# Chunked attention and two MoE layers on one core: a TensorE order written by hand at the entry, earlier weight transfers, and the column sums of w_out as matrix products

## The chip, the cores and the metric

The kernel runs on one core of one Trainium2 chip. The metric is the time of one execution in device microseconds; the profile comes from one profiled execution on the same kind of core. In the profile PE is TensorE's matrix products and PEld its weight loads, DVE is VectorE, ACT is ScalarE, POOL is GpSimd, and SP is the queue that issues most DMA transfers.

## The reference

Three layers follow each other. Chunked attention over 3072 tokens (4 batches of 768, 8 heads of 64): each chunk of 32 queries sees 16 keys to its left, its own 32, 8 to its right, and 8 memory keys. Its output, 3072 rows of 512, goes through a dense layer with 2048 hidden features, and that through a layer of 8 experts in which each token is assigned to one expert, each expert taking exactly 384 tokens.

```python
def _moe_ref(x, w_in, w_out, s, b):
    h = x @ w_in
    r = np.maximum(h, 0.0)
    g = s * (r * r) + b
    return (g @ w_out).astype(np.float32)
```

The dense layer is the one that the change is about. `w_in` and `w_out` come as float64. Since `b` is added to each of the hidden features, its share of the output is `b` times the column sums of `w_out`, one row of 512 numbers for all tokens.

## The kernel before

Tokens go in 24 tiles of 128, and two tiles make a group of 256 columns; there are twelve groups.

Attention of one tile (`stages`, from line 180) is a chain between the engines: TensorE transposes keys (`pk`) and queries (`pq`), ScalarE copies them (`kT`, `qT`), VectorE and ScalarE set up the key windows (`kwin`), TensorE makes the scores (`sc`), VectorE takes maxima and subtracts (`mx`, `sm`), ScalarE takes the exponential, TensorE transposes (`pp`), ScalarE copies (`pT`), TensorE multiplies with the values (`po`, from the buffers `vw`), VectorE divides (`den`, `xr`), TensorE transposes (`px`), ScalarE rounds the result (`xT` high part, line 240) and VectorE keeps the remainder (`xT` low part, line 241).

The dense layer works in units (group, f), f from 0 to 15, each for 128 hidden features. `gemm1` makes twelve matrix products of 256 columns (line 316, tile `ph`: four slices of the model dimension, and for each high times high, high times low, low times high). ScalarE takes relu (line 319), square and rounding; VectorE keeps the low part `g` (line 324). `gemm2` adds the unit into the two output tiles of its group with six products of 512 columns (line 345), three units later (LAG). `ph` comes from a PSUM pool with two buffers, the output tiles from one with four.

The weights arrive as float64 and are converted while the first units run (`convert`, line 265). A piece is 128 columns of `w_in` or 128 rows of `w_out`, 512 KB; there are 32, and three buffers `raw` hold them. For each, ScalarE makes a scaled copy `y` (line 277), VectorE does three integer operations (lines 278, 280, 281), ScalarE rounds the high part (line 262) and GpSimd subtracts for the low part (line 263). For pieces of `w_out` GpSimd also adds `y` into `wsum` (line 290), and one product with ones (line 397) sums that over the partitions once groups 0 and 1 are through.

Groups 0 and 1 run together, group 1 behind group 0, and from group 2 on the groups follow each other, with the attention of later tiles between. The order on TensorE is written out for tiles 0 and 1 only (`begin` in `manual_schedule`); behind that a scheduler places instructions by its own estimate of the times. The order of SP's transfers is written out through the whole entry (`begin`, `startup`, `feed`). All queues run in order: an instruction that waits holds everything behind it on its engine.

Of the kernel before, what the change touches and what calls it, by code (L numbers as in the profile page):

```python
# [18 lines left out]
P = 128  # L19
# [5 lines left out]
def kernel(ctx, tc, q, k, v, mem_k, mem_v, w_in, w_out, moe_s, moe_b,  # L25
# [33 lines left out]
    nc.gpsimd.memset(wsum, 0.0)  # L59
# [48 lines left out]

    vb = [None, None]
# [44 lines left out]
    def k_transpose(t):  # L154
        x = k_raw.pop(t)
        pk = psa[0].tile([P, HP, P], F32, tag="pa", name=f"pk{t}")
        for hp in range(HP):
            nc.tensor.transpose(pk[:, hp, :], x[:, 2 * hp:2 * hp + 2, :].rearrange("p h d -> p (h d)"), ident)
        kT[t] = at.tile([P, HP, P], F32, tag="kT", name=f"kT{t}", bufs=3)
        nc.scalar.activation(kT[t], pk, AF.Copy)  # L160

    def windows(t):
        b = t // TPB
# [3 lines left out]
        cp = (nc.vector if t < 2 * GT else nc.gpsimd).tensor_copy  # L167
        for c in (1, 2):
            nc.scalar.activation(kwin[:, :, c, 0:W], x[:, :, c * CH - LEFT:c * CH - LEFT + W], AF.Copy)
# [9 lines left out]

    def stages(t):  # L180
        first, last = t % TPB == 0, t % TPB == TPB - 1
# [6 lines left out]
        nc.scalar.activation(qT, pq, AF.Copy)  # L188
        windows(t)
        sc = [psa[0].tile([P, HP, KW], F32, tag="pa", name=f"sc{t}_{i}") for i in range(2)]  # L190
# [10 lines left out]
        for par in range(2):  # L201
            if first:
                nc.vector.memset(sc[par][0:CH, :, 0:LEFT], -1.0e30)
            if last:
                nc.vector.memset(sc[par][P - CH:P, :, W - RIGHT:W], -1.0e30)
            nc.vector.tensor_reduce(mx[:, par, :], sc[par], axis=AX.X, op=ALU.max)
            nc.vector.tensor_tensor(sm[:, :, par, :], sc[par],
                                    mx[:, par, :, None].to_broadcast([P, HP, KW]), op=ALU.subtract)
        nc.scalar.activation(sm, sm, AF.Exp, scale=scale)
# [4 lines left out]
        (nc.scalar.copy if t < 2 * GT else nc.vector.tensor_copy)(pT, pp)  # L214
# [12 lines left out]
        for par in range(2):  # L227
            nc.vector.tensor_scalar(den[:, par, :], po[par][:, :, D], 1e-9, None, op0=ALU.add)
        nc.vector.reciprocal(den, den)
        for par in range(2):  # L230
            nc.vector.tensor_tensor(xr[:, :, par, :], po[par][:, :, 0:D],
                                    den[:, par, :, None].to_broadcast([P, HP, D]), op=ALU.mult)
# [7 lines left out]
        nc.scalar.activation(hi, px, AF.Copy)  # L240
        nc.vector.tensor_tensor(lo, px, hi.bitcast(F32), op=ALU.subtract)
# [17 lines left out]
    st = sctx.enter_context(tc.tile_pool(name="st", bufs=2))  # L259

    def split(c, hi, lo, i):
        nc.scalar.activation(hi, c, AF.Copy)  # L262
        nc.gpsimd.tensor_tensor(lo, c, hi.bitcast(F32), op=ALU.subtract)

    def convert(src, a, n, hi, lo, i):

        if src.dtype == F32:
# [4 lines left out]
        raw = st.tile([P, a, n, 2], I32, tag="raw", name=f"raw{i}", bufs=3)  # L272
        nc.sync.dma_start(raw.rearrange("p a f w -> p a (f w)"),
                          src.bitcast(I32).rearrange("(a p) f -> p a f", p=P))
# [13 lines left out]
    def load_wout(f):  # L288
        y = convert(w_out[f * P:(f + 1) * P, :], 1, DM, wout_ap3(0, f), wout_ap3(1, f), 2 * f + 1)
        nc.gpsimd.tensor_tensor(wsum, wsum, y[:, 0, :], op=ALU.add)  # L290
# [18 lines left out]

    def gemm1(j, f):  # L310
        ph = ps_h.tile([P, GN], F32, tag="ph", name=f"ph{j}_{f}")
# [21 lines left out]
    def gemm2_(j, f):  # L333
        nonlocal ps_o, ps_l
        if (j, f) == (3, 0):
            octx.close()
            ps_o, ps_l = (actx.enter_context(tc.tile_pool(name=n, bufs=k, space=PSUM, reuse_waits="tile"))
                          for n, k in (("ps_o3", 3), ("ps_l", 1)))
# [54 lines left out]
    def load_wg():  # L393
        ones = xp[0].tile([P, P], F32, tag="x2", name="onesP")
        nc.vector.memset(ones, 1.0)
        ps = psa[0].tile([P, DM], F32, tag="pa", name="pws")
        nc.tensor.matmul(ps, ones, wsum, start=True, stop=True)
# [632 lines left out]
```

## Time and profile before

| | |
|---|---|
| time, median of 3 runs | 1112.98 us (1112.59 to 1114.03) |
| the profiled execution's own time | 1110.14 us |
| its span | 1108.4 us |
| TensorE busy | 1017.7 us, 92% |
| VectorE busy | 776.3 us, 70% |
| ScalarE busy | 474.1 us, 43% |
| GpSimd busy | 230.9 us, 21% |

A busy TensorE in this table is one whose products stand in its pipeline one behind the other; it may still run at a lower clock. The 8% in which it idles lies at the two ends of the program: in the first 140 us, where weights are still being converted, and in the last 400, where tokens are routed to the experts. The change is about the first.

### The profile page before, as it was taken

The page shows a single profiled execution, that of the slowest core. Times are in us where ns is not written, and L with a number is a line of the kernel's source. Part 1 is how long each engine was busy: PE and PEld are TensorE (multiplying, and loading weights), DVE is VectorE, ACT ScalarE, POOL GpSimd, SP SyncE. Part 2 cuts the span into 40 slices and gives each one's busy share as a digit, 9 for nine tenths or more (in the row PEclk, how much of TensorE's full clock was granted, in tenths as well). Part 3 has the DMA queues.
Part 4 walks back from the last instruction along what each step waited for, and adds up shares of the span by engine and source line. Part 5 has one row for each costly group of instructions (what it writes and reads, how often), then busy time and mean ns, then how long its engine had stood idle before and what let it go on. Part 6 is the DMA issues. An engine that isn't in the chain of part 4 may idle for free.

```text
span 1108.4 us, 25066 instructions
## 1 busy us (share of the span) xinstructions
PE 1017.7 (92%) x9397; PEld 889.8 (80%) x9397; DVE 776.3 (70%) x2979; ACT 474.1 (43%) x1055; POOL 230.9 (21%) x257
## 2 busy tenths in 40 slices
PE   4678899999999999999999999958989899987997
PEld 3557788888888898989898888747878787877986
DVE  4898846984889598989698643579677667774210
ACT  4656554444444454545444445034244143333421
POOL 2566530000121011121120000010112020135631
PEclk9989999999999999999999998959999899998999
DMA  7966503121212121212211000144346063353500
GB/s 168 229 185 167 132 19 127 46 71 38 54 23 73 37 66 47 50 36 62 58 37 37 1 1 20 51 149 153 113 126 202 18 200 95 116 144 113 161 29 29
DMA packets 157913, 96.56 MB, mean 87 GB/s; under 512 B 100312, under 2 KB 141272, under 8 KB 157664
## 3 DMA queue, kind: packets, MB, share of 16 engines
q1 hardware_dynamic: 153376, 81.32, 27.2%
q0 software_dynamic: 3840, 12.59, 3.5%
q8 instruction: 74, 1.21, 0.5%
q10 hardware_dynamic: 576, 1.05, 0.3%
q14 instruction: 47, 0.39, 0.1%
HBM read 82.33 MB, written 12.60 MB: 86 GB/s over the span
## 4 chain that ended last, share of the span: by engine, by line
PE 63%; DVE 21%; issue 7%; DMA 5%; ACT 1%; POOL 1%; SPq 1%; POOLq 0%; DVEq 0%; ACTq 0%
PE ph L316 19%; PE o L345 19%; PE pg L910 8%; PE pf L889 7%; DVE lsc L378 5%; DVE e L839 4%; PE pc L708 2%; DVE u L280 2%; DMA raws<-in_moe_w_dram 2%; DVE g L324 1%; PE po L221 1%; PE sc L195 1%; DVE y L281 1%; DVE rounded L795 1%; PE px L870 1%
## 5 line engine op out<-in xcount | busy, mean ns | idle before, releaser
L316 PE MATMUL ph<-xT,win 128*128 128x256 f32 x2304 | 323.7, 288 | 10.0 <-ACT win L262 7.2
L316 PEld LDWEIGHTS ph<-xT,win 128*128 128x128 f32 x2304 | 301.6, 192 | 28.4 <-ACT win L262 10.6
L345 PE MATMUL o<-wout,g 128*128 128x512 f32 x1038 | 275.0, 400 | 4.4 <-DVE g L324 2.2
L345 PEld LDWEIGHTS o<-wout,g 128*128 128x128 f32 x1038 | 184.4, 189 | 39.4 <-DVE g L324 3.4
L378 DVE SCALAR_TENSOR_TENSOR lsc<-x,wgb 128x128 int8<-128x128 f32 x640 | 158.3, 299 | 3.3 <-DMA wgb<-wgd 1.1
L319 ACT ACTIVATE r<-ph 128x256 f32<-128x256 f32 x192 | 72.9, 382 | 172.0 <-PE ph L316 160.6
L889 PE MATMUL pf<-xgh,e 128*128 128x384 f32 x512 | 140.8, 349 | 0.0
L910 PE MATMUL pg<-e,hh 128*128 128x512 f32 x384 | 130.5, 415 | 0.0
L838 ACT ACTIVATE e<-raws 128x512 fp32r<-128x512 f32 x128 | 79.6, 630 | 93.8 <-DMA raws<-in_moe_w_dram 92.8
L324 DVE TENSOR_TENSOR g<-r,g 128x256 fp32r<-128x256 f32 x173 | 80.2, 465 | 53.7 <-ACT g L323 50.9
L889 PEld LDWEIGHTS pf<-xgh,e 128*128 128x128 f32 x512 | 96.5, 196 | 5.1 <-issue 3.0
L378 DVE SCALAR_TENSOR_TENSOR lsc<-c,wgb 128x512 int8<-128x512 f32 x128 | 98.9, 773 | 2.1
L910 PEld LDWEIGHTS pg<-e,hh 128*128 128x128 f32 x384 | 74.5, 198 | 19.1 <-issue 5.5
L889 PE MATMUL pf<-xgl,e 128*128 128x384 f32 x256 | 88.7, 346 | 0.0
L897 DVE SCALAR_TENSOR_TENSOR hl<-pf,hh 128x384 fp32r<-128x384 f32 x64 | 35.3, 553 | 69.0 <-ACT hh L896 69.0
L320 ACT ACTIVATE r<-r 128x256 f32<-128x256 f32 x192 | 79.7, 418 | 5.4
L910 PE MATMUL pg<-e,hl 128*128 128x512 f32 x192 | 79.4, 414 | 0.0
L323 ACT ACTIVATE g<-r 128x256 fp32r<-128x256 f32 x173 | 71.6, 416 | 5.0 <-PE o L345 0.3
L859 POOL DMA_INDIRECT xg<-x2d,vw x24 | 24.7, 1030 | 200.1 <-DVE vw L702 127.2
L917 POOL DMA_INDIRECT out_dram<-qk,vw x24 | 25.6, 1068 | 186.8 <-ACT qk L916 174.6
L839 DVE TENSOR_TENSOR e<-raws,e 128x512 fp32r<-128x512 f32 x96 | 60.2, 682 | 3.4 <-PE pg L910 1.3
L896 ACT ACTIVATE hh<-pf 128x384 fp32r<-128x384 f32 x64 | 30.9, 485 | 71.6 <-PE pf L889 70.2
(216 smaller groups left out, 1358.2 us busy)
## 6 DMA issues: line engine op xcount, KB each, us to landing
raws<-in_moe_w_dram SPq DMA_DIRECT2D x128, 256.0 KB
vw<-in_v_dram SPq DMA_DIRECT2D x176, 56.0 KB
raw<-in_moe_w_in_dram SPq DMA_DIRECT2D x16, 512.0 KB
raw<-in_moe_w_out_dram SPq DMA_DIRECT2D x16, 512.0 KB
k<-in_k_dram SPq DMA_DIRECT2D x24, 256.0 KB
q<-in_q_dram SPq DMA_DIRECT2D x24, 256.0 KB
x2d<-x SPq DMA_DIRECT2D x20, 256.0 KB
wgb<-wgd SPq DMA_DIRECT2D x1, 2048.0 KB
```

Of the source, the lines that this page charges most:

```text
L316: nc.tensor.matmul(ph, win_ap(a, kk, f), x[:, kk, :], start=(n == 0), stop=(n == 3 * KD - 1))
L319: nc.scalar.activation(r, ph, AF.Relu)
L320: nc.scalar.activation(r, r, AF.Square)
L323: nc.scalar.activation(hi, r, AF.Copy)
L324: nc.vector.tensor_tensor(lo, r, hi.bitcast(F32), op=ALU.subtract)
L345: nc.tensor.matmul(PO[j][u], g[:, u * P:(u + 1) * P], wout_ap(a, f), start=(f == 0 and n == 0), stop=(f == FT - 1 and n == 2))
L378: nc.vector.scalar_tensor_tensor(sc[:, z], a[:, z], 1.0, b[:, z], op0=ALU.mult, op1=ALU.mult, accum_out=acc[:, i:i + 1])
L838: nc.scalar.activation(hi, raw, AF.Copy)
L839: (V if ph < E - 2 else nc.gpsimd).tensor_tensor(lo, raw, hi.bitcast(F32), op=ALU.subtract)
L889: nc.tensor.matmul(pf, w[:, kk, f * P:(f + 1) * P], x[:, kk, :], start=(n == 0), stop=(n == 3 * KD - 1))
L897: V.scalar_tensor_tensor(lo, pf, 0.0, hi.bitcast(F32), op0=ALU.max, op1=ALU.subtract)
L910: nc.tensor.matmul(pg, h[:, j * P:(j + 1) * P], w[:, f, :], start=(n == 0), stop=(n == 3 * FT2 - 1))
```

## The change

Five things are done together.

1. The first three pieces of `w_in` are fetched at points written into `begin`, before the values of tiles 0 and 1; the rest of the transfers of the entry is in a new order too.
2. VectorE's and ScalarE's work for the attention of tiles 0 to 3 is given to the scheduler with high priority (`Ahead`).
3. The order on TensorE is written out for tiles 2 and 3 and for the first eighteen units: a unit, a step of attention, a `gemm2`, a step.
4. Group 1 starts six units behind group 0 instead of ten.
5. GpSimd's additions into `wsum` go. `column_sums` multiplies a matrix of ones with both parts of each piece of `w_out` on TensorE, two products of 512 columns for each of 16 pieces, into one PSUM bank (`psw`). The two `ph` buffers, which lay in two banks, become two halves of one bank (`halves`) until group 3, where the old pool returns; in the built program the first product of each unit in `halves` waits for ScalarE's relu of the unit right before it.

```diff
@@ constants, helpers
     wsum = const.tile([P, DM], F32, name="wsum")
-    nc.gpsimd.memset(wsum, 0.0)
...
+    class Ahead:
...
+        def __getattr__(self, name):
+            def call(*args, **kw):
+                with tc.high_priority():
+                    return getattr(self.engine, name)(*args, **kw)
+            return call
+
+    def engines(t):
+        return (Ahead(nc.vector), Ahead(nc.scalar)) if t < 2 * GT else (nc.vector, nc.scalar)
...
@@ k_transpose, windows and stages: nc.vector and nc.scalar become V and S throughout
+        V, S = engines(t)
...
-        nc.scalar.activation(qT, pq, AF.Copy)
+        S.activation(qT, pq, AF.Copy)
         windows(t)
+        if GT <= t < 2 * GT:
+            yield
...
+            scaled[t] = V.tensor_tensor(xr[:, :, par, :], po[par][:, :, 0:D],
+                                        den[:, par, :, None].to_broadcast([P, HP, D]), op=ALU.mult)
...
@@ conversion of the weights
+    onesr = st.tile([P, P], F32R, name="onesr", bufs=1)
+    nc.vector.tensor_scalar(onesr, ident, 0.0, 1.0, op0=ALU.mult, op1=ALU.add)
...
+    def fetch(src, a, n, i):
+        raw = st.tile([P, a, n, 2], I32, tag="raw", name=f"raw{i}", bufs=3)
+        nc.sync.dma_start(raw.rearrange("p a f w -> p a (f w)"),
+                          src.bitcast(I32).rearrange("(a p) f -> p a f", p=P))
+        return raw
+
+    def fetch_win(f):
+        if w_in.dtype != F32:
+            raws[2 * f] = fetch(w_in[:, f * P:(f + 1) * P], KD, P, 2 * f)
...
+        raw = raws.pop(i) if i in raws else fetch(src, a, n, i)
...
     def load_wout(f):
-        y = convert(w_out[f * P:(f + 1) * P, :], 1, DM, wout_ap3(0, f), wout_ap3(1, f), 2 * f + 1)
-        nc.gpsimd.tensor_tensor(wsum, wsum, y[:, 0, :], op=ALU.add)
+        convert(w_out[f * P:(f + 1) * P, :], 1, DM, wout_ap3(0, f), wout_ap3(1, f), 2 * f + 1)
+
+    def column_sums(f):
+        for a in range(2):
+            nc.tensor.matmul(psw[0], onesr, wout_ap(a, f), start=(f + a == 0), stop=(f == FT - 1 and a == 1))
...
@@ gemm1, gemm2_, load_wg
-        ph = ps_h.tile([P, GN], F32, tag="ph", name=f"ph{j}_{f}")
+        if ps_h is None:
+            half[0] ^= 1
+            ph = halves[:, half[0], :]
+        else:
+            ph = ps_h.tile([P, GN], F32, tag="ph", name=f"ph{j}_{f}")
...
-            ps_o, ps_l = (actx.enter_context(tc.tile_pool(name=n, bufs=k, space=PSUM, reuse_waits="tile"))
-                          for n, k in (("ps_o3", 3), ("ps_l", 1)))
+            ps_h, ps_o, ps_l = (actx.enter_context(tc.tile_pool(name=n, bufs=k, space=PSUM, reuse_waits="tile"))
+                                for n, k in (("ps_h", 2), ("ps_o3", 3), ("ps_l", 1)))
...
-        nc.tensor.matmul(ps, ones, wsum, start=True, stop=True)
-        nc.vector.tensor_scalar(wsum, ps, b_col, None, op0=ALU.mult)
+        nc.vector.tensor_scalar(wsum, psw[0], b_col, None, op0=ALU.mult)
...
@@ begin, startup, the loop over units
+        fetch_win(0)
...
+        fetch_win(1)
         load_v(0)
+        fetch_win(2)
...
-        for _ in range(3):
+        for i in range(3):
             next(run0, None)
+            if i < 2:
+                feed(1)
+            next(run1, None)
+        with tc.issue_after(scaled[1].ins):
             feed(1)
-            next(run1, None)
...
-    def startup():
-        for t in range(2, 2 * GT):
-            load_q(t)
-            feed(1)
-            load_k(t + 1)
-            feed(1)
-            load_v(t)
+    def attention_steps():
+
+        for t in range(GT, 2 * GT):
             k_transpose(t + 1)
-            attention(t)
+            run = stages(t)
+            next(run)
+            if t + 1 < 2 * GT:
+                load_k(t + 2)
+            yield
+            for z in run:
+                yield
+            yield
...
+        psw = [ps_w.tile([P, DM], F32, name="psw")]
+        halves = ps_w.tile([P, 2, GN], F32, name="halves")
+        load_q(GT)
+        feed(1)
+        load_k(GT + 1)
+        load_v(GT)
+        feed(1)
+        load_q(GT + 1)
+        load_v(GT + 1)
...
-    units = [(0, f) for f in range(10)]
+    SKEW = 6
+    units = [(0, f) for f in range(SKEW)]
     for f in range(FT):
-        units += [(1, f)] + ([(0, f + 10)] if f + 10 < FT else [])
+        units += [(1, f)] + ([(0, f + SKEW)] if f + SKEW < FT else [])
...
+            if j == 0:
+                feed(2)
             gemm1(j, f)
+            if i < 2 * FT:
+                next(steps, None)
...
-                gemm2(*pend.pop(0))
+                gemm2(*pend[0])
+                z = pend.pop(0)
+                if z[0] == 0:
+                    column_sums(z[1])
+            if 2 < i < 2 * FT or i == 1:
+                next(steps, None)
...
+    with tc.manual_schedule(engines={mybir.EngineType.SP}):
+        with tc.manual_schedule(engines={mybir.EngineType.PE}):
+            for _ in range(18):
+                next(run_products)
```

How the instructions stand in the built programs, at two places. First VectorE behind the softmax of tiles 0 and 1 (`den_408` and `xr_409` belong to tile 0 before, `den_409`, `xr_410` to tile 0 and `den_425`, `xr_426` to tile 1 in the change; `u`, `y` and `raw` belong to weight pieces). Before:

```order
L278 TENSOR_SCALAR u_309<-raw_306 128x512
L280 SCALAR_TENSOR_TENSOR u_309<-y_308,u_309 128x512
L281 SCALAR_TENSOR_TENSOR y_308<-y_308,u_309 128x512
L278 TENSOR_SCALAR u_367<-raw_364 128x512
L228 TENSOR_SCALAR den_408<-po_0_330 128x4
L228 TENSOR_SCALAR den_408<-po_1_331 128x4
L280 SCALAR_TENSOR_TENSOR u_367<-y_366,u_367 128x512
L229 RECIPROCAL den_408<-den_408 128x8
L278 TENSOR_SCALAR u_427<-raw_424 128x512
L281 SCALAR_TENSOR_TENSOR y_366<-y_366,u_367 128x512
L231 TENSOR_TENSOR xr_409<-po_0_330,den_408 128x4x64
L231 TENSOR_TENSOR xr_409<-po_1_331,den_408 128x4x64
```

In the change:

```order
L312 SCALAR_TENSOR_TENSOR u_368<-y_367,u_368 128x512
L313 SCALAR_TENSOR_TENSOR y_367<-y_367,u_368 128x512
L116 TENSOR_SCALAR den_409<-po_0_333 128x4
L116 TENSOR_SCALAR den_409<-po_1_334 128x4
L116 RECIPROCAL den_409<-den_409 128x8
L116 TENSOR_TENSOR xr_410<-po_0_333,den_409 128x4x64
L116 TENSOR_TENSOR xr_410<-po_1_334,den_409 128x4x64
L116 TENSOR_SCALAR den_425<-po_0_375 128x4
L116 TENSOR_SCALAR den_425<-po_1_376 128x4
L116 RECIPROCAL den_425<-den_425 128x8
L116 TENSOR_TENSOR xr_426<-po_0_375,den_425 128x4x64
L116 TENSOR_TENSOR xr_426<-po_1_376,den_425 128x4x64
```

The conversions of `raw_364` and `raw_424` stood between the operations of tile 0; now both tiles' divisions stand together. Next on VectorE in the change come `u_442<-raw_439` and `u_468<-raw_465`, and behind them the two low parts of `xT`.

Second, TensorE where tile 3's attention ends and group 1 begins (`px_754` before and `px_1002` in the change are tile 3's last transposes; `g_6` and `g_2` are the hidden parts of units 6 and 2 of group 0). Before:

```order
L345 MATMUL o_0_1098<-wout_78,g_6_1174 128x512
L345 MATMUL o_1_1099<-wout_78,g_6_1174 128x512
L316 MATMUL ph_9_1236<-xT_0_420,win_75 128x256
L316 MATMUL ph_9_1236<-xT_1_421,win_75 128x256
L345 MATMUL o_0_1098<-wout_80,g_6_1174 128x512
L345 MATMUL o_0_1098<-wout_78,g_6_1175 128x512
L345 MATMUL o_1_1099<-wout_80,g_6_1174 128x512
L345 MATMUL o_1_1099<-wout_78,g_6_1175 128x512
L235 MATMUL px_754<-ident,xr_748 128x128 x4
L158 MATMUL pk_1494<-ident,k_1482 128x128 x4
L316 MATMUL ph_9_1236<-xT_0_420,win_77 128x256
L316 MATMUL ph_9_1236<-xT_0_420,win_75 128x256
```

In the change:

```order
L386 MATMUL o_1_790<-wout_79,g_2_696 128x512
L386 MATMUL o_1_790<-wout_77,g_2_697 128x512
L325 MATMUL psw<-wout_77,onesr 128x512
L325 MATMUL psw<-wout_79,onesr 128x512
L255 MATMUL px_1002<-ident,xr_996 128x128 x4
L172 MATMUL pk_1469<-ident,k_1457 128x128 x4
L357 MATMUL halves<-xT_0_785,win_73 128x256
L204 MATMUL pq_1476<-ident,q_1447 128x128 x4
L357 MATMUL halves<-xT_1_786,win_73 128x256
L357 MATMUL halves<-xT_0_785,win_75 128x256
```

Tile 3's last transposes came when unit 9 of group 0 was under way; now they come behind unit 5, and the first unit of group 1 (`halves<-xT_0_785`) stands right behind them. From group 4, unit 6 on TensorE's order is that of before, word for word but for numbers, up to the end.

## Rows read from the trace of the kernel before

**Rows 1.** Stretches: length, busy us by engine (instructions), TensorE clock, DMA share, GB/s.

```profile
38.85:87.53 48.68, 39.08 (x449) 32.58 (x448) 44.34 (x73) 31.21 (x67) 29.46 (x23) 0.89 0.75 196
87.53:132.64 45.11, 38.77 (x343) 30.92 (x342) 40.91 (x55) 24.89 (x59) 28.84 (x24) 1.00 0.59 164
...
169.46:312.00 142.54, 142.28 (x1508) 126.83 (x1506) 111.62 (x659) 65.39 (x157) 10.78 (x25) 1.00 0.26 69
```

**Rows 2.** TensorE by time: start, length, line, tiles, count [idle before, releaser].

```profile
31.06 1.09 PE L235 MATMUL px<-ident,xr 128*128 128x128 f32 x4 [8.19 <-DVE xr L231]
...
38.85 4.39 PE L316 MATMUL ph<-xT,win 128*128 128x256 f32 x23
```

**Rows 3.** VectorE in order of time, four instructions of the entry.

```profile
24.88 0.43 DVE L278 TENSOR_SCALAR u<-raw 128x512 int32<-128x512 int32 x1 [6.20 <-DMA raw<-in_moe_w_in_dram]
...
26.30 0.69 DVE L281 SCALAR_TENSOR_TENSOR y<-y,u 128x512 int32<-128x512 int32 x1
...
40.33 0.41 DVE L278 TENSOR_SCALAR u<-raw 128x512 int32<-128x512 int32 x1
...
87.53 0.68 DVE L241 TENSOR_TENSOR xT<-px,xT 128x512 fp32r<-128x512 f32 x1
```

**Rows 4.** SP's queue in order of time: issues of transfers.

```profile
29.51 5.54 SPq L150 DMA_DIRECT2D vw<-in_v_dram  x8
...
35.60 0.52 SPq L273 DMA_DIRECT2D raw<-in_moe_w_in_dram  x1
```

**Rows 5.** Chain that ended last, two stretches: start, length, what.

```profile
20.27 8.92 DMA raw<-in_moe_w_out_dram
...
161.35 1.40 PE o L345 x6
...
162.74 1.44 PE ph L316 x12
...
168.41 0.86 PE pws L397 x2
...
173.13 0.44 PE pk L158 x4
...
178.14 0.79 PE sc L195 x53
```

**Rows 6.** VectorE by line, 20 to 145 us: count, busy us, mean ns, idle.

```profile
L280 DVE SCALAR_TENSOR_TENSOR u<-y,u 128x512 int32<-128x512 int32 x31 | 33.6, 1084 | 9.5 <-ACT y L277 9.5
...
L281 DVE SCALAR_TENSOR_TENSOR y<-y,u 128x512 int32<-128x512 int32 x31 | 28.0, 903 | 1.5 <-DVE den L228 0.4
...
L278 DVE TENSOR_SCALAR u<-raw 128x512 int32<-128x512 int32 x31 | 22.9, 739 | 7.7 <-DMA raw<-in_moe_w_in_dram 6.4 <-DMA raw<-in_moe_w_out_dram 1.0
...
L324 DVE TENSOR_TENSOR g<-r,g 128x256 fp32r<-128x256 f32 x23 | 15.3, 680 | 0.3 <-ACT g L323 0.3
...
L231 DVE TENSOR_TENSOR xr<-po,den 128x256 f32<-128x256 f32 x10 | 3.8, 417 | 0.1
```

**Rows 7.** GpSimd by line, 0 to 145 us.

```profile
L263 POOL TENSOR_TENSOR win<-y,win 128x512 fp32r<-128x512 f32 x16 | 23.1, 1446 | 42.9 <-ACT win L262 42.9
...
L290 POOL TENSOR_TENSOR wsum<-wsum,y 128x512 f32<-128x512 f32 x15 | 21.8, 1456 | 16.0 <-DVE y L281 16.0
```

**Rows 8.** Waits from 38 to 150 us: total, times, longest.

```profile
ACT win L262 <- DVE y L281: 20.4, 11, 3.4
...
ACT y L277 <- POOL wout L263: 2.9, 3, 2.2
```

**Rows 9.** ScalarE by line, 20 to 145 us.

```profile
L262 ACT ACTIVATE win<-y 128x512 fp32r<-128x512 f32 x15 | 9.5, 630 | 20.8 <-DVE y L281 20.7
...
L319 ACT ACTIVATE r<-ph 128x256 f32<-128x256 f32 x24 | 8.5, 373 | 7.4 <-DVE g L324 6.7 <-PE ph L316 0.7
```

**Rows 10.** Two stretches of 5 us; DMA share and GB/s stand last.

```profile
15.00:20.00 5.00, 2.77 (x72) 2.16 (x72) 2.44 (x9) 2.75 (x6) 0.00 (x0) 1.00 0.39 82
...
45.00:50.00 5.00, 5.00 (x35) 4.56 (x34) 4.41 (x11) 4.28 (x12) 2.46 (x2) 1.00 1.10 326
```


## What the change does to the time: the prediction

> **What bounds the kernel now.** I read the table of stretches first, then TensorE's and VectorE's instructions in order of time, then the chain that ended last, and at the end the groups by line. The table is cut at four events: TensorE's first unit (38.85 us), the low part of tile 3's `xT` (87.53), the end of TensorE's last wait for a weight (132.64), and the first product of group 2 (169.46). In the first two stretches VectorE is busy 44.34 of 48.68 us and 40.91 of 45.11, TensorE 39.08 and 38.77; behind 169.46 TensorE is busy 142.28 of 142.54, VectorE 111.62 [rows 1]. So VectorE sets the pace to 132 us and TensorE from there on. Since the change leaves TensorE's order as it was from group 4 on, what it gains or loses by group 2 stays in the total, and I forecast one number: how much earlier or later group 2 begins.
>
> Before 38.85 us the limit is another. TensorE sits 8.19 us until VectorE's `xr` [rows 2], and VectorE had itself sat 6.20 us, until 24.88, for a weight piece that stands ahead of the divisions in its order [rows 3]. The next piece, of `w_out`, took 8.92 us from issue to landing [rows 5]. In 15 to 20 us the DMA engines were busy for a share of 0.39 only, and in 45 to 50 us they were full [rows 10]: transfers come too late at first and then all at once.
>
> **The ledger of before.** A unit's `gemm1` takes 1.44 us and its `gemm2` 1.40; a tile's attention takes two times 0.79 (`sc`, and `po` like it) and four times 0.44 for the transposes, 3.3 [rows 5]. From 38.85 to 169.46, 130.6 us, TensorE does 32 `gemm1` (46.1), 29 `gemm2` (40.6), four tiles (13.4), the product with ones (0.86) and one group of transposes (0.44): 101.4. The other 29.2 are not work: 15.9 of idle time in two stretches [rows 1] and 13.3 of slow products. The first 23 took 4.39 us [rows 2], at 12 in 1.44 they would take 2.8, and the granted clock of that stretch was 0.89 [rows 1].
>
> **Part by part.**
>
> *Early transfers and attention first, at the entry.* With its data there, the piece that VectorE waited for 6.20 us is converted before tile 1's softmax, and the divisions of both tiles stand together. Behind the last `po` come two divisions of some 1.5 us each (twice 0.417 [rows 6] and small operations), the transposes, two roundings and two low parts of 0.68 [rows 3], with the first operations of two pieces (0.43 and 0.69 [rows 3]) between. `po` ended at 31.06 − 8.19 = 22.9 us [rows 2]; I put its end one to two us later, since 1 MB more stands in the queues ahead of the values (at 326 GB/s [rows 10] 3.2 us, of which the idle share at 15 to 20 us takes about half). So 24.5 for `po`, 3 for the divisions, 1.1 for the last transposes [rows 2], 1.4 for two low parts, one us for the pieces between: about 31. I take 30.5, with 28 and 34 as bounds. Before it was 38.85.
>
> *The same lead further on.* Between tiles 2 and 3 SP has to issue eight small transfers of values per tile, which took 5.54 us, and only behind them the piece with which VectorE's full stretch began: issued at 35.60 [rows 4], used at 40.33 [rows 3]. In the new order both groups of eight stand ahead of it and three other pieces come sooner, and I put its use at 38. So of eight us at the entry two are left where VectorE's long stretch begins; the rest waits for transfers.
>
> *GpSimd without `wsum`.* Fifteen additions of 1456 ns in this stretch go [rows 7]. They matter through VectorE: its integer operations mean 1084, 903 and 739 ns, and singly they took 0.69 and 0.43 when alone [rows 3, 6]. Over 31 pieces that is 33.6 − 21.4, 28.0 − 21.4 and 22.9 − 13.3, and for the low parts `g` 15.3 − 9.4 [rows 6]: 34 us of stretching, beside 46 instructions of GpSimd (16 and 15 low parts, 15 additions), 0.75 each. An addition can't cost VectorE more than its own length, 1.46. I take 1.0, nearer to 0.75, since VectorE also loses time before such an instruction starts. From 40.33 to the low part of tile 3's `xT` at 88.2 [rows 3] VectorE took 47.9 us. In the change the same stretch of its order holds six additions less beside it (6.0) and three low parts `g` less, of 0.68 (2.0), and ScalarE waits less for `y` buffers, which those additions held (2.9 in all [rows 8]; 0.9 of it here). So 39 us, and group 1 can begin at 38 + 39 = 77 instead of 88.
>
> *The written order, six units behind.* By 77 TensorE has done six `gemm1`, three `gemm2`, three pairs of column sums, two tiles and a transpose: 8.6 + 4.2 + 1.4 + 6.7 + 0.4 = 21.3. It idles for much of that time, behind softmaxes that now stand with little work in front; that costs nothing, since 77 is set by VectorE.
>
> *Column sums.* 32 products at a sixth of 1.40 [rows 5] are 7.5 us; the product with ones, 0.86, goes. Bounds: nothing for those that fall into waits, 7.5 for all. Six of the 32 come before 77 and are hidden; the rest counts in full, since from there TensorE's own work is the longer path. All of TensorE's work is then 101.4 − 0.86 + 7.5 = 108.0, and 86.7 of it lies behind 77.
>
> *The sum.* 77 + 86.7 + waits. In the like stretch of before TensorE idled 6.3 us [rows 1]; with a third of GpSimd's load gone and group 1 beside group 0 I take 2.5, between 0 and 6.3. Group 2 then begins at 166.2 instead of 169.46, 3.3 us earlier: a profiled execution of 1110.14 − 3.3 = 1106.8. The median of the runs is 2.84 above the profiled execution, so 1109.7.
>
> **One bank for two halves.** Before, relu was read from a buffer of its own bank, and its 373 ns [rows 9] lay beside the next unit's products. Now the next `gemm1` starts only when relu of the last one is through; what stands between them is a `gemm2` of 1.40 us and often a pair of column sums, 0.47. So relu is covered as long as ScalarE takes it at once. The Trainium skill ("PSUM — Partial Sum Buffer", the section on bank collisions) says that two engines must be kept apart by bank, whichever columns of it they touch; by that rule two halves are no double buffer and the wait can't go. No run shown so far has it, since `ph` had two banks; what it could cost is worked out as the third case below.
>
> **The rivals.**
>
> *A: the sum above*, 1109.7, with 1107 to 1112 as its own range. For it: each term has a row. Against it: it is a small difference of large numbers. Chance 0.38.
>
> *B: VectorE gets freer than I count, and TensorE is the limit early.* At 1.46 for an addition six of them give 8.8 instead of 6.0, and an entry two us sooner would carry through: group 1 at 72, no waits behind it: 72 + 86.7 = 158.7, 10.8 earlier, 1102. For it: the chain of waits runs through VectorE nearly all the way to 132. Against it: from 40 to 50 us the DMA engines are full [rows 10], and that doesn't change. Chance 0.17.
>
> *C: the single bank makes it slower.* ScalarE's rounding of a weight piece waits for VectorE, 11 times for 20.4 us, 1.85 each, longest 3.4 [rows 8]. If relu stands behind such a one, the next `gemm1` starts 1.85 + 0.63 (the rounding) + 0.37 (relu) [rows 9] = 2.9 us after the last one ended, against a cover of 1.87: a loss of 1.0 each time, 2.5 at the longest. Eight us over the 26 units behind 77 make 77 + 86.7 + 2.5 + 8 = 174.2, 4.7 later, 1117.7. It decides once the sum of TensorE's waits for relu passes the 3.3 us that A has won. Chance 0.25.
>
> *D: the lead is given back to the transfers.* The piece at 35.60 leaves SP hardly earlier, VectorE's long stretch begins at 39.5, and an addition costs 0.75: 39.5 + 47.9 − 4.5 − 2.0 = 80.9 for group 1, and 80.9 + 86.7 + 2.5 = 170.1: 0.6 later, 1113.6, no difference that can be told. For it: VectorE's idle time at the entry is waiting for transfers [rows 3]. Chance 0.2.
>
> **How the numbers follow.** About 0.2%, 2.2 us, is what a measurement of this kernel tells from no change. B is faster, and of A four fifths, since its upper end lies inside the 2.2: 0.17 + 0.3 = 0.47. The last fifth of A and four fifths of D are the same: 0.08 + 0.16 = 0.24. C and the rest of D are slower: 0.29. The range goes from just below B, 1101, to just above C, 1119.
>
> **What would show it.** Right: the first `halves` product at about 30 us; tile 3's low part at 77; group 2 at 166; the mean of line 280's operation well below 1084 ns; no GpSimd instruction but the low parts and copies. TensorE's waits for relu decide between A and C: below 3 us in all for A, above 7 for C. If VectorE's long stretch begins at 39.5 or later, D. Wrong: if the time before group 2 stays as it was and the total differs, the effect lies behind group 4, where I have none.

## The result: 1.1% slower, and the profile after

The changed kernel takes 1124.77 us (1121.03 to 1126.42) beside 1112.78 for the kernel before on the same chip: a ratio of 1.0107, 95% interval 1.0084 to 1.0131, 9 to 15 us. The forecast was 1109.7, the range ended at 1119: wrong, on the wrong side.

First the stretches of the changed kernel, cut like [rows 1]: from the eleven products that remain of the first unit to tile 3's last low part, to the end of the weights, and on.

```profile
36.80:86.43 49.63, 31.19 (x393) 26.90 (x393) 42.22 (x76) 30.80 (x63) 22.48 (x19) 0.78 0.85 224
86.43:132.00 45.57, 41.69 (x360) 34.27 (x361) 39.20 (x59) 28.96 (x64) 22.63 (x19) 1.00 0.53 152
132.00:182.62 50.62, 50.62 (x486) 43.85 (x484) 14.61 (x37) 22.00 (x53) 5.43 (x14) 1.00 0.23 68
```

Up to group 1's first unit TensorE works 31.19 us instead of 39.08, and idles 18.4 instead of 9.6, at a clock of 0.78 instead of 0.89. Behind that it idles less than before (3.9 us to 132, against 6.3). Its waits from 20 us to the start of group 2, in us, times and longest, after and then before:

```profile
PE pp L232 <- ACT sm L116: 10.5, 4, 4.3
PE px L255 <- DVE xr L116: 7.7, 4, 4.6
PE halves L357 <- ACT xT L116: 5.0, 2, 4.7
PE sc L215 <- ACT qT L116: 3.9, 2, 3.0
PE halves L357 <- ACT r L360: 3.5, 4, 1.1
```

```profile
PE px L235 <- DVE xr L231: 11.5, 4, 8.2
PE ph L316 <- ACT win L262: 7.2, 5, 3.1
PE o L345 <- DVE g L324: 2.2, 2, 1.4
```

Before, TensorE behind tile 1 waited for weights: it had used up what was converted. Now it waits for steps of attention (softmax, divisions, queries), and no unit waits for a weight: converted pieces lie ready. TensorE in order of time shows the place:

```profile
34.76 0.58 PE L357 MATMUL halves<-xT,win 128*128 128x256 f32 x1 [4.74 <-ACT xT L116]
36.80 2.71 PE L357 MATMUL halves<-xT,win 128*128 128x256 f32 x11 [1.46 <-DVE xT L116]
...
45.87 1.18 PE L215 MATMUL sc<-kwin,qT 64*32 64x64 f32 x64 [3.00 <-ACT qT L116]
51.35 1.12 PE L232 MATMUL pp<-ident,sm 128*128 128x128 f32 x4 [4.30 <-ACT sm L116]
52.12 2.91 PE L357 MATMUL halves<-xT,win 128*128 128x256 f32 x12
...
83.58 0.63 PE L255 MATMUL px<-ident,xr 128*128 128x128 f32 x4 [2.00 <-DVE xr L116]
...
185.45 1.60 PE L357 MATMUL halves<-xT,win 128*128 128x256 f32 x12
```

A unit at 52.12 takes 2.91 us where the one at 185.45 takes 1.60, and stands behind waits of 3.00 and 4.30. When tile 3's last transposes come (83.58; before 85.39) TensorE has done six `gemm1` and three `gemm2`; before, nine and seven. That is 4.3 and 5.6 us less by [rows 5], against three pairs of column sums more and 1.8 us of lead. Weights were not what kept more units from standing there: GpSimd, which ends a conversion, was through with the seventh piece of `w_out` and the tenth of `w_in` by then. Its instructions in order of time:

```profile
79.54 1.29 POOL L285 TENSOR_TENSOR wout<-y,wout 128x512 fp32r<-128x512 f32 x1 [4.53 <-ACT wout L284]
80.82 1.43 POOL L285 TENSOR_TENSOR win<-y,win 128x512 fp32r<-128x512 f32 x1
```

Group 2 starts at 185.45 instead of 169.46, 4.5 us of it because two `gemm2` and steps of tiles 6 and 7 now stand ahead.

A mark behind which both orders are the same is better than the start of group 2: tile 13's last transposes, at 386.22 us before and 396.62 after. So 10.4 us are lost by then. From there to the end the same instructions took 722.2 us before, 728.0 in the profiled run of the change, and 720 to 727 in the kernels below, with no relation to what was changed in front that I could find. I therefore read each kernel by its ratio and by this mark. The mark comes from one profiled execution of each kernel, so its own scatter is not known; I make nothing of a difference of one us.

### The profile page after: what moved, and what is told of

It reads as the page before. It is cut to its first block, busy times and chain, and to the rows that moved or that the text cites. A ratio compares the mean times of both kernels' runs of the same rounds, so it can differ in the third digit from the quotient of the medians.

```text
span 1124.6 us, 25106 instructions
## 1 busy us (share of the span) xinstructions
PE 1025.7 (91%) x9427; PEld 898.0 (80%) x9427; DVE 766.2 (68%) x2979; ACT 476.2 (42%) x1055; POOL 205.0 (18%) x240
## 4 chain that ended last, share of the span: by engine, by line
PE 63%; DVE 18%; DMA 7%; issue 6%; ACT 2%; POOL 2%; SPq 1%; POOLq 0%; DVEq 0%; ACTq 0%
PE o L386 19%; PE ph L357 15%; PE pg L977 7%; PE pf L956 7%; PE halves L357 5%; DVE lsc L419 5%; DVE e L906 3%; DMA raws<-in_moe_w_dram 3%; DMA raw<-in_moe_w_in_dram 3%; PE pc L775 2%; PE sc L215 1%; PE po L241 1%; DVE u L312 1%; DVE y L313 1%; DVE g L365 1%
## 5 line engine op out<-in xcount | busy, mean ns | idle before, releaser
L357 PE MATMUL ph<-xT,win 128*128 128x256 f32 x1680 | 231.4, 284 | 0.0
L357 PEld LDWEIGHTS ph<-xT,win 128*128 128x128 f32 x1680 | 218.3, 190 | 10.3
L360 ACT ACTIVATE r<-ph 128x256 f32<-128x256 f32 x140 | 53.5, 382 | 137.7 <-PE ph L357 133.6
L357 PE MATMUL halves<-xT,win 128*128 128x256 f32 x624 | 90.9, 296 | 10.4 <-ACT xT L116 5.0
L357 PEld LDWEIGHTS halves<-xT,win 128*128 128x128 f32 x624 | 83.0, 199 | 15.7 <-ACT xT L116 5.5
```

Of the source, the lines that this page charges most:

```text
L357: nc.tensor.matmul(ph, win_ap(a, kk, f), x[:, kk, :], start=(n == 0), stop=(n == 3 * KD - 1))
L360: nc.scalar.activation(r, ph, AF.Relu)
```

## The experiments

The last two columns are read from the profiled runs; units are whole `gemm1` and `gemm2` standing ahead of tile 3's last transposes. The ratios are to the kernel before as it ran beside each of them: 1111.2 us for e1 to e4, 1113.8 for e5 to e8, 1111.4 to 1111.5 for e9 to e14.

| kernel | ratio to before (95%) | units ahead | tile 3 last transposes | tile 13 against before |
|---|---|---|---|---|
| before | 1 | 9, 7 | 85.39 | 0 |
| the change | 1.0107 (1.0084–1.0131) | 6, 3 | 83.58 | +10.4 |
| e1 sums on GpSimd | 1.0183 (1.0163–1.0203) | 6, 3 | 86.77 | +19.8 |
| e2 before, sums on TensorE | 0.9994 (0.9978–1.0009) | 10, 8 | 84.50 | −0.8 |
| e3 scheduler's order | 1.0087 (1.0071–1.0103) | 6, 6 | 83.23 | +6.8 |
| e4 ten units | 1.0081 (1.0065–1.0097) | 6, 3 | 82.92 | +8.6 |
| e5 both | 1.0009 (0.9992–1.0026) | 10, 8 | 88.36 | +2.5 |
| e6 fifth piece moved | 1.0119 (1.0100–1.0137) | 6, 3 | 83.35 | +14.2 |
| e7 one step a unit | 1.0038 (1.0024–1.0053) | 8, 5 | 86.62 | +5.8 |
| e8 before, late sums | 1.0076 (1.0055–1.0097) | 10, 7 | 81.62 | +9.4 |
| e9 no priorities | 1.0107 (1.0083–1.0130) | 6, 3 | 81.60 | +11.2 |
| e10 old entry | 1.0049 (1.0031–1.0067) | 6, 3 | 78.78 | +5.7 |
| e11 before, six units | 1.0075 (1.0055–1.0096) | 6, 6 | 87.22 | +11.0 |
| e12 before, sums, priorities | 1.0001 (0.9985–1.0017) | 10, 8 | 83.71 | −1.5 |
| e13 four pieces moved | 1.0061 (1.0041–1.0081) | 6, 3 | 81.21 | +7.9 |
| e14 written order, old entry | 1.0062 (1.0040–1.0084) | 8, 5 | 87.05 | +6.2 |

**e1, e2: the column sums.** e1 puts them back on GpSimd. e2 does nothing else of the change, except that `ph` has to go into the one bank of two halves to make room.

```diff
-                if z[0] == 0:
-                    column_sums(z[1])
...
+        nc.gpsimd.tensor_tensor(wsum, wsum, y[:, 0, :], op=ALU.add)
```

> The changed kernel with the column sums of w_out back on GpSimd (16 additions into wsum and one product with ones; the 32 products psw go). Theory W (written order and the work of the column sums): behind 86 us TensorE is the limit, so 13 of 16 pairs of products at about 0.5 us come off its path, 6 to 7 us; before 86 us VectorE runs beside 6 additions more and gives 2 to 4 back. Time about 1121, 8 above the kernel before. Rival V (VectorE sets the pace all along, also in the changed kernel): the 15 additions slow VectorE by 0.75 to 1 us each, and the time goes up, 1127 or more. If the column sums were the whole of the loss: 1113.

> The kernel before with nothing but the column sums on TensorE (and with it the one bank of two halves, which makes room for psw). Theory W: TensorE idles 15.9 us between 39 and 133 us there, so most of the 7.5 us of products is hidden and VectorE loses 15 additions beside it; time 1108 to 1114. Rival S (the column sums cost their full length wherever they stand): 6.6 above before, 1119 to 1120.

My first theory held the sums for half of the loss, and e1 refutes it: without them on TensorE the change is worse, by 9.4 us at tile 13; at 1132.32 us it is where rival V had it. The additions slow VectorE beyond tile 3 too: from 86.43 to 132 us TensorE idles 7.3 us in e1 at a clock of 0.86, in the change 3.9 at 1.00. VectorE's means in the change, 20 to 145 us, answer to [rows 6]; below them the same operations in e1.

```profile
L312 DVE SCALAR_TENSOR_TENSOR u<-y,u 128x512 int32<-128x512 int32 x30 | 24.8, 831 | 5.9 <-ACT y L309 5.8
L310 DVE TENSOR_SCALAR u<-raw 128x512 int32<-128x512 int32 x30 | 16.9, 564 | 8.7 <-DMA raw<-in_moe_w_in_dram 7.6 <-DMA raw<-in_moe_w_out_dram 0.8
```

```profile
L310 DVE SCALAR_TENSOR_TENSOR u<-y,u 128x512 int32<-128x512 int32 x29 | 27.7, 962 | 9.9 <-ACT y L307 9.7
L308 DVE TENSOR_SCALAR u<-raw 128x512 int32<-128x512 int32 x30 | 24.9, 832 | 8.8 <-DMA raw<-in_moe_w_in_dram 7.6 <-DMA raw<-in_moe_w_out_dram 1.0
```

On the kernel before (e2) the sums are worth nothing that can be told, as theory W had it: VectorE's last operation of a conversion starts at 124.63 instead of 144.22 us, and no time comes of it. That the 32 products take what the relief gives is the likely reading; no run separates the two.

**e3, e4, e5: the written order and the distance.**

```diff
-        with tc.manual_schedule(engines={mybir.EngineType.PE}):
-            for _ in range(18):
-                next(run_products)
+        for _ in range(18):
+            next(run_products)
...
-    SKEW = 6
+    SKEW = 10
```

> The changed kernel in which the first eighteen units and tiles 2 and 3 stand on TensorE in the scheduler's order instead of the written one; transfers, entry, priorities, column sums and six units' distance stay. Theory W: in the written order TensorE stood 19.9 us between 34.8 and 86.4 us behind softmaxes while converted pieces lay ready; the scheduler fills this with units, and 5 to 9 us come back: 1116 to 1120. Rival T (transfers at the entry are the cause, the order is not): 1123 to 1126.

> The changed kernel with group 1 ten units behind group 0 instead of six. Theory W: up to tile 3's last transposes at 83.6 us the written order is the same word for word, and behind that TensorE is the limit whichever group it works on: within 2 us of the changed kernel, 1123 to 1126. Rival K (the short distance is the cause, since group 0's units that could have filled the waits come too late): 1114 to 1118.

> Both of the last two together: the changed kernel with ten units' distance and with the scheduler's order on TensorE for units and tiles 2 and 3. What is left of the change is then the entry, the priorities and the column sums. Theory U (the loss is unit work of group 0 that was ready and didn't stand before tile 3's last transposes: 6 gemm1 and 3 gemm2 instead of 10 and 7, about 11 us): at 85 us nine or ten gemm1 and seven gemm2 are done again, and the time is that of the kernel before within 3 us: 1111 to 1114. Rival T (the entry and its transfers carry the rest): 1117 or more, no better than either alone.

e3 (first edit) and e4 (second) each give a little back, and both medians, 1120.96 and 1119.46 us, fell between the theory and its rival: e3 gained less than theory W had it, e4 more. Both rest at six `gemm1` ahead of tile 3, e3 because the scheduler follows the program's order of units, e4 because the written order has no place for more. At tile 13 e4 is 1.8 us better than the change. Together (e5) the units are back, and so is the time, within what can be measured by the ratio; at tile 13 it is 2.5 us behind the kernel before. This is the clearest result.

**e7, e11: the same from two sides.** e7 leaves the order written, at ten units' distance, with one attention step a unit from the fifth on; e11 gives the kernel before only the distance of six.

```diff
@@ e7, with SKEW = 10
-            if i < 2 * FT:
+            if i < 4:
                 next(steps, None)
@@ e11, in the kernel before
-    units = [(0, f) for f in range(10)]
+    units = [(0, f) for f in range(6)]
...
-        units += [(1, f)] + ([(0, f + 10)] if f + 10 < FT else [])
+        units += [(1, f)] + ([(0, f + 6)] if f + 6 < FT else [])
```

> The changed kernel with ten units' distance and with one attention step behind each unit from the fifth unit on instead of two; still a written order. Theory U: at tile 3's last transposes eight gemm1 and five gemm2 are done instead of six and three, at the price of one to two us for tile 3; 3 to 4 us less than with ten units' distance alone (1119.5): 1115 to 1117. Rival (VectorE's conversions come too late for more units there, and TensorE waits for win): tile 3 later by 4 us or more, 1120 to 1124.

> The kernel before with nothing but group 1 six units behind group 0 instead of ten. Theory U: units 6 to 9 of group 0 no longer stand ahead of tile 3's last transposes, four gemm1 and some gemm2 less are done at 87 us, and part of it is won back from waits behind: 4 to 8 us slower, 1116 to 1120 (before about 1112). Rival (VectorE and the transfers set the pace to 132 us whatever TensorE does): 1110 to 1114.

e7 has the eight and five units of theory U and is faster than e4, as forecast (1.0038 against 1.0081); its median, 1117.87 us, is above the 1115 to 1117 set down for it. It makes tile 3 3.7 us later than e4, where one to two were expected, and is still 2.8 us better at tile 13. e11 came out as theory U had it, at 1119.86 us: the distance alone, in the scheduler's order, costs 11.0 us at tile 13, as much as the whole change there, and 0.75% by the ratio, where the change costs 1.07%. Tile 3 is at 87.22.

**e6, e10, e13: the entry.** e10 takes the old order of transfers and feeds; e6 and e13 keep the new transfers and move conversions behind attention on ScalarE and VectorE (e13 keeps the sixth piece's transfer where it was and moves four conversions). Of the change's three early fetches the third, issued at 16.80 us, stands behind the values of tile 0 and ahead of those of tile 1.

```diff
@@ e10
-        fetch_win(0)
...
             next(run0, None)
-            if i < 2:
-                feed(1)
+            feed(1)
             next(run1, None)
...
@@ e6, e13
-        feed(1)
+        with tc.issue_after(high[1].ins), tc.issue_after(low[1].ins):
+            feed(1)
...
@@ e13
+            if i == 0:
+                with tc.issue_after(quer[GT].ins), tc.issue_after(keyw[GT].ins):
+                    feed(3)
```

> The changed kernel with one edit: ScalarE's and VectorE's work on the fifth weight piece (issued at 24.0 us, landed at 33.1) stands behind the rounding and the low part of tile 1's xT instead of ahead of them. Theory U: the first unit starts at about 31 instead of 34.8 to 36.8, but tiles 2 and 3 are set by transfers and VectorE, tile 3's low part stays at 84 to 86, and the time stays within 2 us of the changed kernel: 1121 to 1125. Rival E (the late entry is the loss; five us at the first unit carry through): 1117 to 1120.

> The changed kernel without the three early fetches of w_in and with the pieces fed between the steps of tiles 0 and 1 as before. Theory U: tile 3's last transposes stay at 83 to 86 us, the loss stays, 1121 to 1126 (before about 1112). Rival T (a megabyte of weights ahead of the values is what delays the attention): 1116 to 1119.

> The changed kernel with its transfers, but with the work of four weight pieces moved in ScalarE's and VectorE's order: the fifth behind tile 1's xT, the sixth to eighth behind tile 2's queries and key windows. Theory O (an engine that takes its instructions in order waits 3 to 4 us each time for a piece that has not landed, with attention work behind it): tile 2's scores start at 41 to 42 instead of 45.9, tile 3's last transposes come at 78 to 80 instead of 83.6, and the time falls by 3 to 5 us to 1.006 to 1.008 of the kernel before. Rival B (the bytes are late whatever stands in front): tile 3's transposes at 83 or later, and 1.010 or more of the kernel before.

In e6 the first unit starts at 29.80 and 32.04 instead of 34.76 and 36.80, and nothing is gained: the second unit then waits 4.50 us for a relu that stands on ScalarE behind the sixth piece. Its mark at tile 13 is 3.8 us worse: TensorE's waits for relu up to 180 us sum to 10.1 instead of 3.5, and the clock between 86 and 132 us was 0.91. So e6 trades one stall for another and doesn't tell what an early first unit by itself would be worth. e10 contradicted me: with an entry that brings the first unit no sooner (37.26) tile 3 comes 4.8 us earlier and 4.7 us come back. ScalarE shows a part of why, first in the change, then in e10:

```profile
40.70 0.58 ACT L116 ACTIVATE kT<-pk 128x512 f32<-128x512 f32 x1
41.18 0.41 ACT L364 ACTIVATE g<-r 128x256 fp32r<-128x256 f32 x1
44.66 0.68 ACT L309 ACTIVATE y<-raw 128x512 f32<-128x512 f32 x1 [3.07 <-DMA raw<-in_moe_w_in_dram]
45.24 0.58 ACT L116 ACTIVATE qT<-pq 128x512 f32<-128x512 f32 x1
```

```profile
41.38 0.58 ACT L116 ACTIVATE kT<-pk 128x512 f32<-128x512 f32 x1
41.85 0.41 ACT L364 ACTIVATE g<-r 128x256 fp32r<-128x256 f32 x1
42.16 0.59 ACT L116 ACTIVATE qT<-pq 128x512 f32<-128x512 f32 x1
```

In the change a piece that has not landed stands ahead of tile 2's queries, which TensorE had transposed from 40.16 on. The same happened at 33.07 ahead of tile 1's `xT`: the chain that ended last runs there through a transfer of 8.97 us.

```profile
24.01 8.97 DMA raw<-in_moe_w_in_dram
33.07 0.67 ACT y L309
33.74 0.49 ACT xT L116
```

The Trainium skill ("PSUM — Partial Sum Buffer", the section on engine and sequencer instructions) says that the queues of ScalarE and VectorE are strictly first in, first out; these rows agree. e13 moves the stalls out of the way. Tile 2's scores start at 39.17, sooner than theory O had it, but the next stall takes over, on VectorE ahead of the softmax:

```profile
42.00 1.28 DVE L116 COPY kwin<-kT 128x192 f32<-128x192 f32 x1
46.91 0.43 DVE L310 TENSOR_SCALAR u<-raw 128x512 int32<-128x512 int32 x1 [3.63 <-DMA raw<-in_moe_w_in_dram]
47.25 0.42 DVE L365 TENSOR_TENSOR g<-r,g 128x256 fp32r<-128x256 f32 x1
47.59 0.75 DVE L116 TENSOR_TENSOR sm<-sc,mx 128x256 f32<-128x256 f32 x2
```

Tile 3 comes 2.4 us earlier, and 2.5 of the entry's 4.7 us are back, though the seventh and eighth pieces are issued 1.7 us later than in the change. Its ratio, 1.0061, is in theory O's range; its tile 3, at 81.21, lies between theory and rival. So about half of the entry's price is pieces in front of attention. Whether the rest is the same again or the transfers themselves stays open.

**e9, e12: the priorities.** e9 takes them out of the change, e12 puts them on e2.

```diff
-        return (Ahead(nc.vector), Ahead(nc.scalar)) if t < 2 * GT else (nc.vector, nc.scalar)
+        return nc.vector, nc.scalar
```

> The changed kernel without the high priorities for VectorE's and ScalarE's attention work of tiles 0 to 3. Theory U: the written TensorE order now waits longer for softmaxes that stand behind conversions, tile 3's last transposes come 2 us or more later, and the time is 1125 to 1131 against a kernel before of about 1112. Rival P (the priorities hold up the conversions and cost time themselves): 1119 to 1122.

> The kernel before with the column sums on TensorE and with the high priorities for the attention of tiles 0 to 3, nothing else of the change. With the sums alone it was level with the kernel before (ratio 0.9994). Theory U: tile 3 is done 2 to 3 us sooner, ten units stand before it as in the kernel before, and the time is 1107 to 1110 (before about 1112). Rival P (the conversions fall behind, and units wait for weights): 1112 to 1116.

They are worth nothing that can be told (0.8 and 0.7 us at tile 13). Both forecasts missed: e9 has the ratio of the change, and its tile 3 comes 2.0 us sooner instead of later, without gain at tile 13; e12 is level with the kernel before.

**e8, e14: two attempts at something better.** e8 is the kernel before with the sums behind the last conversion, 16 additions on GpSimd and 15 on VectorE; e14 is e7 with the old entry.

```diff
+        with tc.issue_after(last[0].ins):
+            for f in range(FT):
+                nc.gpsimd.tensor_tensor(wsum, wsum, wout_ap(0, f).bitcast(F32), op=ALU.add)
...
+        for f in range(2, FT):
+            nc.vector.tensor_tensor(wlow, wlow, wout_ap(1, f).bitcast(F32), op=ALU.add)
```

> The kernel before, with its order and two banks for ph, but the column sums neither on GpSimd beside the conversions nor as 32 products: behind the last conversion GpSimd adds up the 16 high parts and VectorE the 16 low parts, and two products with ones end it (1.7 us). Theory G (VectorE is slowed by GpSimd's additions, and the 32 products cost TensorE their time behind 87 us): the conversions end near 125 us instead of 139, TensorE has 6 us less work than with the 32 products, and the time is 1104 to 1108. Rival H (behind 87 us TensorE was the limit already, VectorE's relief is worth nothing): 1110 to 1113. Rival L (the late additions hold up wsum, and with it the release of the o banks at the start of group 2): 1113 or more.

> The changed kernel with the old entry, ten units' distance and one attention step behind each unit from the fifth unit on; order on TensorE still written. Theory U (no loss in the written order as such: what counts is how many units stand ahead of tile 3's transposes and when these come): the parts add up, 4.7 for the entry, 1.8 for the distance and 2.9 for the steps of 10.4 at tile 13's transposes, so that 1 us is left: 0.999 to 1.003 of the kernel before. Rival (the written order loses by itself, where the scheduler fills waits that a fixed order can't): 1.004 or more.

e8 came out at 1123.0 us, far from theory G's 1104 to 1108. Its conversions ended sooner as hoped (VectorE's last operation of them starts at 125.72), but the late additions stand ahead of tile 5's softmax on VectorE, which is not the place that rival L named:

```profile
157.04 1.11 PE L212 MATMUL pp<-ident,sm 128*128 128x128 f32 x4 [9.87 <-ACT sm L209]
```

The parts did not add up in e14: with eight units in front tile 3 is at 87.05, the entry's gain there is gone, and the result is about e7's. Its ratio of 1.0062 is where the forecast had put the rival, that a written order loses by itself. With eight and five units ahead it also stands short of the nine and seven of the kernel before, so it doesn't tell the two apart, and that rival stays open. Nor do the units tell everything: five kernels with six and three of them, the change among them, lie between +5.7 and +11.2 us at tile 13, and e6 at +14.2. No kernel here beats the one before.

## Why the prediction was wrong

**The step that failed** is the lead that was to pay for the written order: "So 39 us, and group 1 can begin at 38 + 39 = 77 instead of 88", and what the next step built on it: "It idles for much of that time, behind softmaxes that now stand with little work in front; that costs nothing, since 77 is set by VectorE." The sum did carry the units left for later, in the 86.7 us behind 77. It set against them a lead of eleven us. The lead measured 1.8: tile 3's low part was through at 86.37 instead of 88.21. What the order gave up for it, three `gemm1` and four `gemm2` whose pieces lay converted, 9.9 us by [rows 5], was then paid for behind tile 3, where TensorE had only 3.9 us of idle time left. That the idling was not free is what e5, e7 and e11 show: units put back ahead of tile 3 bring time back, and six units' distance in the kernel before costs 11.0 us at tile 13.

By the runs, order and distance together make 7.9 us at tile 13 (the change to e5), and the entry 4.7 (e10). These shares don't add: with eight units ahead the old entry gives nothing (e7 +5.8, e14 +6.2), and the sums, worth nothing that can be told in the kernel before (e2), are worth 9.4 in the change (e1). That 7.9 and 4.7, with 0.8 and 0.7 given back (e2, e12), come to 11.1 beside 10.4 measured is therefore luck as much as account.

**The time of 77 for tile 3.** It came at 86.37, 9.4 us late. The first term, VectorE's long stretch from 38, is off by 6.6 us: but for 0.25 us at 67.44, VectorE last sits idle for a piece until 44.60. That piece left SP at 40.51 only, behind two groups of eight transfers of values, which took 8.47 and 4.43 us to issue; in the kernel before the first such group took 5.54 [rows 4].

```profile
44.60 0.43 DVE L310 TENSOR_SCALAR u<-raw 128x512 int32<-128x512 int32 x1 [2.47 <-DMA raw<-in_moe_w_in_dram]
...
85.68 0.69 DVE L116 TENSOR_TENSOR xT<-px,xT 128x512 fp32r<-128x512 f32 x1
```

Case D's sign, a stretch that begins at 39.5 or later, was there; its 1113.6 us had too little of it. The 39 us from there to the end of tile 3's low part took 41.8. The first unit at 30.5 (28 to 34) came at 34.76 and 36.80: the last `po` ended at 27.57 instead of 24.5, and I had put at nothing the 3.57 us for which ScalarE waits for the fifth piece ahead of tile 1's `xT`. In e6, where the first unit came at 29.80, nothing was gained, since another stall followed.

**GpSimd without `wsum`** was right: by the means above VectorE's two operations save 0.253 and 0.175 us in 31 pieces and the low parts `g` (611 ns instead of 680) 1.6 us in all, 14.9 over 15 additions, 1.0 each. The change alters other things too; e2, which takes the additions away and little else, gives nearly the same. There line 278's operation (279 in e2) saves 0.280 us and line 280's (281) 0.178, line 281's (282) loses 0.076, and `g` saves 2.1 us in all: 14.0, or 0.9 each.

```profile
L282 DVE SCALAR_TENSOR_TENSOR y<-y,u 128x512 int32<-128x512 int32 x31 | 30.3, 979 | 1.8 <-DVE den L227 0.4
L281 DVE SCALAR_TENSOR_TENSOR u<-y,u 128x512 int32<-128x512 int32 x31 | 28.1, 906 | 7.2 <-ACT y L278 7.2
L279 DVE TENSOR_SCALAR u<-raw 128x512 int32<-128x512 int32 x31 | 14.2, 459 | 8.5 <-DMA raw<-in_moe_w_in_dram 7.1 <-DMA raw<-in_moe_w_out_dram 1.0
```

**The stretch behind tile 3.** I had 89.2 us (86.7 and 2.5); it took 99.0, from 86.43 to 185.45. Some 4.5 is work that moved ahead of the mark, waits were 3.9 instead of 2.5, and the rest, about 4, are products that take longer than the ledger has them: a unit behind a short group of `sc`, for one, takes 1.53 us from start to start (90.13 to 91.66) instead of 1.44. Why they do stays open. The 13.3 us of slow products of the ledger I had left out altogether, and this is what they cost: in the kernel before they make 5.6 of its stretch behind 87.53, worked out in the same way. The 9.4 us from above, 1.4 of waits and these 4 come near the 15.1 by which the time missed the forecast.

**Column sums.** Six of the 32 products came before tile 3, as counted. What the other 26 cost by themselves no run isolates. In the kernel before, relief and cost cancel (e2); in the change the relief is the larger (e1). That e2's conversions end 19.6 us sooner and its time stays also speaks against the premise that VectorE alone sets the pace of the kernel before to 132 us.

**Rival C** fell: the waits for relu are 3.5 us over the units, near A's bound of 3, and the loss lies elsewhere. With two banks they were 1.4, in two waits of up to 0.8. The one bank by itself is not shown to cost anything: e2 and e5, which have it with the scheduler's order, wait 0.9 and 1.6 us. The prediction took from the Trainium skill ("PSUM — Partial Sum Buffer", bank collisions) that two engines are to be kept apart by bank. The wait for relu of the unit right before stands in the built program of every run that has two halves, so none of them tests the rule itself.

## What to carry to other kernels

When an order is written by hand, count for each stretch what the old order had done by its end; an idle bottleneck is free only if nothing ready is left for it. An engine that takes its work in order is held by the first transfer that has not landed, so fetching earlier can pay only if the work on the piece stands behind what others wait for. Read a change to the front of a long program at a mark behind which the orders agree, since the tail scatters by several us.

## What was not expected of the hardware

The low level of TensorE's clock belongs to the price of waiting. Two stretches of the change, one with waits of 3.00 and 4.30 us in and ahead of it, and one of full work:

```profile
45.00:50.00 5.00, 1.18 (x64) 0.94 (x64) 5.00 (x13) 4.53 (x11) 3.10 (x2) 0.50 1.13 302
50.00:55.00 5.00, 3.65 (x22) 3.42 (x24) 4.95 (x9) 2.48 (x5) 1.30 (x2) 0.50 0.76 227
90.00:95.00 5.00, 5.00 (x70) 4.19 (x53) 4.35 (x7) 2.58 (x6) 1.81 (x2) 1.00 0.73 224
```

At 0.50 (1.2 of 2.4 GHz) the twelve products of the unit at 52.12 took 2.91 us, at full clock (185.45) 1.60. A unit at the low level between two steps of attention thus makes the next step later by up to 1.3 us more; this is an estimate from these two rows.
